# Hash-masked attention with a gated MLP: engine order written by hand, packed operand transposes, weights loaded late

## The chip, the cores and the metric

One core of one Trainium2 chip runs the whole program. The metric is device time in microseconds (us) of one execution. In the profile PE is TensorE (matmul), PEld its weight loads, DVE is VectorE, ACT is ScalarE, POOL is GpSimd; SPq is the queue on which the sync engine issues DMA transfers. "PEclk" or "clock" is the share of full clock that TensorE was granted. "Fast" and "slow" are the states of an execution; only fast ones are compared unless the text says otherwise. L190 is line 190 of the kernel in question, so line numbers differ from kernel to kernel.

## The reference, cut to what matters

```python
batch, n_heads, seq, head_dim = (4, 8, 768, 64)
q_bits = (np.einsum('bhsd,dk->bhsk', q, proj) > 0)       # 6 hash bits a token
k_bits = (np.einsum('bhsd,dk->bhsk', k, proj) > 0)
mask = q_bucket[:, :, :, None] == k_bucket[:, :, None, :]
scores = np.where(mask, scale * np.matmul(q, k.transpose(0, 1, 3, 2)), -1e9)
x = softmax(scores) @ v                                  # heads side by side: 3072 x 512
# gated MLP with residual
gelu = gelu_erf(x @ w_gate)                              # 512 -> 1536
ffn_out = (gelu * (x @ w_val)) @ w_out                   # 1536 -> 512
out = x + sigmoid(x @ w_res) * ffn_out
```

Both kernels hold the mask in the matmul: each operand of a score gets seven more rows, six hash bits as plus or minus 0.5 and a constant, so that equal buckets add nothing and unequal ones a large negative number. The work goes by pairs of heads, 16 in all, four to a batch. A pair has nine score chunks; I call one chunk, with its exponential and the value matmuls of the chunk before, a slot. A batch has 36 slots. Its gate/value block (`x @ w_gate`, `x @ w_val`, some 31 us of pure TensorE) comes four slots into the next batch, five in the changed kernel, and for the last batch at the end. The output rows of a batch (`rps`, `fps`) are cut into 30 pieces and slipped between the slots of the next batch. Meanwhile two pairs ahead are prepared: a group.

## The kernel before

The preparation makes one 128x1536 tile an operand, holding data and bits, and transposes it by DMA. All hash matmuls of a group go into one PSUM tile `hs`, and the bits are written before the transpose:

```python
def prep(ps, first=False):
    jobs = [(p, side) for p in ps for side in range(2)]
    hs = mm_ps.tile([P, HT, 32], FP32, tag="mm", name="hs")
    ...
    for h in range(2):
        ...  # VectorE transposes 32x32 blocks of q, k into tt
        for dh in range(2):
            for j, tt in enumerate(t32):
                nc.tensor.matmul(hs[32 * j:32 * j + 32, h * T:(h + 1) * T, :],
                                 projw[:, dh, :], tt[:, :, dh, :], ...)
        yield
    nc.vector.transpose(ht..., hs...)
    for j, x in enumerate(jobs):
        for a in range(4):
            nc.vector.tensor_scalar(nat_of(x)[32 * a:32 * a + 32, :, D:D + NBITS], ht..., ...)
        nc.sync.dma_start_transpose(out=ag, in_=nat_of(x)...)
        aug[x] = ag
        yield
```

The main loop issues a chunk, one step of the preparation, one piece of a row; the tile scheduler orders the engines from there. Weights are loaded from the first slots on:

```python
    scores(p, c)
    ...
    if s in (3, 6, 9, 12, 15) and g < 3:
        load_w()
    next(side, None)
    if b >= 1:
        ...  # one projection piece a slot
        if slot == LEAD - 1:
            ...
            gate_val(b - 1)
```

The row's PSUM tiles `rps` and `fps` and the hash tile share one pool of two buffers: `mm_ps = tc.tile_pool(name="mm_ps", bufs=2, space=PSUM)`.

The softmax here doesn't subtract the row's maximum and nothing guards it: scores larger than these inputs give would overflow.

## Time and profile before

| | before |
|---|---|
| time | 410.14 us median of 2 runs (408.52 to 411.77) |
| profiled execution | span 404.7 us, mean clock 0.920 |
| first score | 21.7 us |
| gate/value block of batch 0 | 98.2 to 132.3 us |
| batch 1, batch 2, batch 3 (from the end of one block to the end of the next) | 84.8, 84.0, 78.1 us |
| after the last block | 25.5 us |

The span is the end of block 0, plus three batches, plus a tail of 25 to 26 us. The profile lines are in the prediction.

### The profile page before, as it was taken

To read this page: it belongs to the slowest core of one execution; us is meant where nothing else is said; L and a number is where in the kernel's file an instruction comes from. 1 tells how busy PE (TensorE), PEld (TensorE's weight loads), DVE (VectorE), ACT (ScalarE), POOL (GpSimd) and SP (SyncE) were. 2 spreads that over 40 slices of the span, in tenths; PEclk is the share of its full clock that TensorE was granted. 3 is DMA by queue.
4 is the path that set the end of the run, shared out by engine and by line. 5 is a ranking of instruction groups with operands and counts; after the bars stand their busy time and mean duration, and the time that the engine had idled before them with its cause. 6 is when DMAs were issued, how large, how long until landed. Compare 5 with 4: busy or idle time off the path is not lost. (4 is left out here: it accounts for less than half of the span.)

```text
span 404.7 us, 7265 instructions
## 1 busy us (share of the span) xinstructions
PE 366.9 (91%) x2944; PEld 202.2 (50%) x2990; DVE 170.7 (42%) x366; ACT 206.9 (51%) x225; POOL 81.5 (20%) x149
## 2 busy tenths in 40 slices
PE   6386969959999999998999999899999999999995
PEld 2133524425566555554665555556655555565542
DVE  3727123715433324734336537443336232333342
ACT  2036534636332877773335886863357788333210
POOL 7456245344300022241000342310000000000000
PEclk9759555865999999999999999999999999999999
DMA  7999999996910048776000973920008221100012
GB/s 220 223 270 245 159 239 285 201 238 142 238 55 2 28 84 188 137 186 202 2 0 2 185 205 85 185 47 2 0 2 158 76 68 47 45 2 0 16 65 78
DMA packets 86177, 46.61 MB, mean 115 GB/s; under 512 B 64640, under 2 KB 83072, under 8 KB 86144
## 3 DMA queue, kind: packets, MB, share of 16 engines
q1 hardware_dynamic: 79488, 40.91, 44.7%
q0 software_dynamic: 6336, 5.24, 8.7%
q8 instruction: 23, 0.38, 0.4%
q14 instruction: 10, 0.08, 0.1%
q10 hardware_dynamic: 320, 0.01, 0.0%
HBM read 29.37 MB, written 6.29 MB: 88 GB/s over the span
## 5 line engine op out<-in xcount | busy, mean ns | idle before, releaser
L260 ACT ACTIVATE e<-sp 128x1024 bf16<-128x1024 f32 x144 | 144.4, 1022 | 83.8 <-PE sp L255 82.4
L255 PE MATMUL sp<-aug,aug 71*128 71x256 bf16 (+1 forms) x384 | 98.2, 362 | 4.3 <-DMA aug<-nat 4.1
L282 ACT ACTIVATE gt<-sp 128x768 bf16<-128x768 f32 x48 | 38.9, 810 | 83.3 <-PE sp L276 83.3
L283 DVE TENSOR_TENSOR hh<-gt,sp 128x768 bf16<-128x768 bf16 x48 | 45.8, 953 | 81.1 <-PE sp L276 81.1
L235 PEld LDWEIGHTS <-e 128*128 128x128 bf16 x1152 | 54.3, 104 | 43.1 <-ACT e L260 24.0
L276 PE MATMUL sp<-x_sb,wg 128*128 128x512 bf16 (+1 forms) x382 | 72.0, 328 | 2.6 <-DMA x_sb<-x_tok 2.1
L300 PE MATMUL fps<-wo,hh 128*128 128x512 bf16 x265 | 71.4, 379 | 1.7 <-issue 0.5
L276 PE MATMUL sp<-x_sb,wv 128*128 128x512 bf16 (+1 forms) x371 | 70.0, 324 | 1.2 <-DVE hh L283 0.5
L235 PE MATMUL av<-va,e 128*128 128x65 bf16 x1152 | 66.1, 204 | 2.2 <-ACT e L260 1.1
L168 DVE STREAM_TRANSPOSE t<-ld 128x384 f32<-128x384 f32 x64 | 33.8, 557 | 43.8 <-DMA ld<-in_q_dram 21.3
L276 PEld LDWEIGHTS <-wg 128*128 128x128 bf16 x384 | 37.5, 98 | 28.1 <-issue 3.9
L255 PEld LDWEIGHTS <-aug 71*128 71x128 bf16 x384 | 34.8, 105 | 32.4 <-issue 6.5
L276 PEld LDWEIGHTS <-wv 128*128 128x128 bf16 x384 | 37.7, 98 | 25.8 <-issue 1.2
L175 PE MATMUL hs<-t,projw 128*32 128x192 f32 x256 | 27.3, 375 | 17.8 <-DVE t L168 11.7
L300 PEld LDWEIGHTS <-hh 128*128 128x128 bf16 x288 | 24.3, 97 | 24.0 <-issue 5.3
L305 DVE SCALAR_TENSOR_TENSOR o<-th,fps 128x512 f32<-128x512 f32 x24 | 16.4, 683 | 39.4 <-PE fps L300 29.6
L186 DVE TENSOR_SCALAR nat<-ht 32x72 bf16<-32x72 f32 x128 | 31.3, 244 | 2.3
L214 DVE RECIPROCAL rec<-av 128x6 f32<-128x6 f32 x32 | 6.0, 187 | 56.0 <-PE av L235 56.0
L138 POOL TENSOR_SCALAR nat<-ld 128x768 bf16<-128x768 f32 x15 | 12.4, 829 | 73.8 <-DMA aug<-nat 73.8
L296 ACT ACTIVATE th<-rps 128x512 f32<-128x512 f32 x24 | 14.3, 596 | 21.0 <-PE rps L293 17.7
L145 POOL CAST va<-ldv 128x768 bf16<-128x768 f32 x16 | 13.2, 822 | 57.2 <-PE av L235 52.5
L293 PE MATMUL rps<-wr,x_sb 128*128 128x512 bf16 x88 | 24.3, 382 | 0.1
(34 smaller groups left out, 152.9 us busy)
## 6 DMA issues: line engine op xcount, KB each, us to landing
ld<-in_q_dram SPq DMA_DIRECT2D x16, 384.0 KB, 4.7
ld<-in_k_dram SPq DMA_DIRECT2D x16, 384.0 KB, 4.6
ldv<-in_v_dram SPq DMA_DIRECT2D x16, 384.0 KB, 5.0
out_dram<-o SPq DMA_DIRECT2D x24, 256.0 KB, 2.1
wg<-in_moe_w_gate_dram POOLq DMA_DIRECT2D x4, 384.0 KB, 9.6
wv<-in_moe_w_val_dram POOLq DMA_DIRECT2D x4, 384.0 KB, 7.1
wo<-in_moe_w_out_dram POOLq DMA_DIRECT2D x3, 512.0 KB, 10.7
aug<-nat SPq DMA_TRANSPOSE x32, 4.9
```

The lines of the kernel that those rows point to most:

```text
L168: nc.vector.transpose(tt.rearrange("p c h n -> p (c h n)"), raw[x][:, h * T:(h + 1) * T].rearrange("p c d -> p (c d)"))
L175: nc.tensor.matmul(hs[32 * j:32 * j + 32, h * T:(h + 1) * T, :], projw[:, dh, :], tt[:, :, dh, :], start=(dh == 0), stop=(dh == 1), tile_p ...
L186: nc.vector.tensor_scalar(nat_of(x)[32 * a:32 * a + 32, :, D:D + NBITS], ht[32 * j:32 * j + 32, :, NBITS * a:NBITS * (a + 1)], 0.0, 0.5, o ...
L235: nc.tensor.matmul(av[p, hi][:, qt, :], e[:, off:off + P], va[:, hi, jt, 0:D + 1], start=False, stop=(jt == T - 1), skip_group_check=True)
L255: nc.tensor.matmul(sp[:, off:off + nq * P], ks[0:KA, hi * T + jt, :], qs[0:KA, hi * T + qt0:hi * T + qt0 + nq, :], start=True, stop=True)
L260: nc.scalar.activation(e, sp, AF.Exp, scale=float(ALPHA))
L276: nc.tensor.matmul(sp[:, c0:c1], w[:, kk, bass.ts(m, P)], xs[:, kk, c0:c1], start=(kk == 0), stop=(kk == KM - 1))
L282: nc.scalar.activation(gt, sp[:, 0:S], AF.Gelu)
L283: nc.vector.tensor_mul(hh[:, m, :], gt, ps[1][:, 0:S])
L293: nc.tensor.matmul(rps, x_sb[b][:, kk, t, :], wr[:, kk, :], start=(kk == 0), stop=(kk == KM - 1))
L300: nc.tensor.matmul(fps, hh[:, m, bass.ts(t, P)], wo[:, m, :], start=(m == 0), stop=(m == KF - 1))
L305: nc.vector.scalar_tensor_tensor(o, th, 1.0, fps, op0=ALU.add, op1=ALU.mult)
```

## The change

Its intent: fewer and smaller DMA transposes, no waits in the first stage, and every engine's order written down instead of left to the scheduler. Two heads share a 128x768 transpose. The second head lands in rows 64 to 127, so VectorE copies it into a tile `second` whose first 64 rows hold its mask rows and zeros. Bits go in by small DMAs ("mask rows") after the transpose. Hashing uses 32x32 tiles, in blocks of 16 matmul instructions that need both buffers of `mm_ps` (the trace records each of them twice, so a block shows as x32). Weights are loaded at slots 20 to 40.

```diff
+    ctx.enter_context(tc.manual_schedule(engines=None))
 ...
+    def move_second(x):
+        nc.vector.tensor_copy(second[x[0] % NM][x[1]][D:P], aug[x][D:P])
 ...
+    def hash_mm(jobs, h, a0):
+        while rows_open:
+            mlp_piece()
+        hs = [mm_ps.tile([P, T, 32], FP32, tag="mm", name="hs") for _ in range(2)]
+        for dh in range(2):
+            for j, x in enumerate(jobs):
+                for i in range(2):
+                    a = a0 + i
+                    nc.tensor.matmul(hs[i][32 * j:32 * j + 32],
+                                     projw[32 * a:32 * a + 32, dh, :],
+                                     t32[x, h][32 * a:32 * a + 32, :, dh, :],
+                                     start=(dh == 0), stop=(dh == 1),
+                                     tile_position=(32 * a, 32 * j))
 ...
+    def mask_rows(jobs, h, sel=None):
 ...
+            dst = aug[x][D:D + NROW] if h == 0 else second[x[0] % NM][x[1]][0:NROW]
+            nc.sync.dma_start(dst, bits[jobs[0]][32 * j:32 * j + NROW, h])
 ...
+        at(s0 + 6, hash_mm, jobs, 0, 0)
+        at(s0 + 7, hash_bits, jobs, 0, 0)
+        at(s0 + 7, hash_mm, jobs, 0, 2)
+        at(s0 + 8, hash_bits, jobs, 0, 2)
+        for i, x in enumerate(jobs):
+            at(s0 + 8 + i // 2, blocks, x, 1)
+            at(s0 + 9 + i // 2, move_second, x)
+        at(s0 + 11, mask_rows, jobs, 0)
+        at(s0 + 10, hash_mm, jobs, 1, 0)
+        at(s0 + 11, hash_bits, jobs, 1, 0)
+        at(s0 + 11, hash_mm, jobs, 1, 2)
+        at(s0 + 12, hash_bits, jobs, 1, 2)
+        at(s0 + 13, mask_rows, jobs, 1)
 ...
-            if s in (3, 6, 9, 12, 15) and g < 3:
-                load_w()
+    for s in (20, 22, 28, 30, 36, 37, 38, 39):
+        at(s, load_w)
+    for s in (40, 40, 40, 40):
+        at(s, load_w)
 ...
+            elif mlp and mlp[0][1] < 5 * T - HELD:
+                mlp_piece()
```

`at(slot, f, ...)` puts a piece of work into a slot; within a slot the order is scores, the listed work, a row piece, then the values of the chunk before. `s0` is the first slot of a group's preparation, 18 slots before its use (15 for the first group).

## The prediction

> **What bounds the kernel now.** I read the page first: busy shares, the 40 slices, the clock row.
>
> ```profile
> PE 366.9 (91%) x2944; PEld 202.2 (50%) x2990; DVE 170.7 (42%) x366; ACT 206.9 (51%) x225; POOL 81.5 (20%) x149
> PE   6386969959999999998999999899999999999995
> ACT  2036534636332877773335886863357788333210
> PEclk9759555865999999999999999999999999999999
> DMA  7999999996910048776000973920008221100012
> ```
>
> TensorE is the busy engine, but the clock row splits the run: for some 100 us it is mostly at half speed, then full to the end. In the first part DMA is full too. The table of 10 us stretches and the DMA queue's timeline say more (columns: length, then busy us and instructions of PE, PEld, DVE, ACT, POOL; clock, DMA share, GB/s).
>
> ```profile
> 40.00:50.00 10.00, 9.89 (x70) 5.05 (x71) 1.93 (x6) 5.12 (x5) 1.59 (x3) 0.50 1.33 166
> 60.00:70.00 10.00, 10.00 (x72) 4.14 (x70) 2.91 (x8) 4.81 (x5) 5.83 (x10) 0.50 1.16 268
> 150.00:160.00 10.00, 9.89 (x110) 5.70 (x109) 4.64 (x10) 7.30 (x8) 2.74 (x5) 1.00 0.68 117
> 50.13 10.44 SPq L191 DMA_TRANSPOSE aug<-nat  x2
> ```
>
> Five exponentials in 10 us early, with TensorE "99% busy" at clock 0.50; later 8 of them plus the projections. Two operand transposes hold the queue for 10.44 us, and loads queue behind them.
>
> Stage limits come from the timeline of TensorE and the chain that ended last.
>
> ```profile
> 98.18 0.83 PE L276 MATMUL sp<-x_sb,wg 128*128 128x512 bf16 x2
> 132.17 0.60 PE L255 MATMUL sp<-aug,aug 71*128 71x256 bf16 x3
> 216.93 0.60 PE L255 MATMUL sp<-aug,aug 71*128 71x256 bf16 x3
> ...
> 301.10 0.43 PE sp L255 x3
> 348.20 1.57 PE sp L276 x9
> 379.28 2.54 PE fps L300 x11
> ```
>
> So: batch 0 with its gate/value block ends at 132.2 (first score at 21.7, block from 98.2); batches 1 and 2 take 84.8 and 84.2; batch 3's attention 47.1; then 31.1 of block and 25.4 of tail. From 132 on TensorE is the bound, nearly without gaps. Its unit costs at full clock, from the chain:
>
> ```profile
> 263.78 1.29 PE fps L300 x6
> 265.07 0.44 PE sp L255 x3
> 265.51 0.24 PE av L235 x8
> ...
> 267.73 0.79 PE hs L175 x16
> ...
> 392.57 0.40 issue
> 392.96 0.70 DVE o L305
> 393.66 0.04 issue
> 393.70 2.75 PE fps L300 x12
> ```
>
> One score chunk (a "slot") is 0.44 + 0.25 = 0.69 us of TensorE and one exponential of 0.99 us (3.97 for four in a row at 78.52). A projection matmul is 0.216. The last four lines show the cost of a full PSUM pool: from the end of one row (392.53) to the next start it is 1.17 us, because VectorE must first read the bank.
>
> **What the Trainium skill says.**
> - "TensorE: Matmul & The Clock Gate", Part 1, has a half/full clock set by activity in free-running windows of about 3.4 us. The trace agrees in kind: half clock at 15.2 after idling from 10.4 to 14.0, full again at 28.9, four windows later. It also warns of a throttle that sticks; here 40 to 73 us stays at 0.50 although TensorE hardly idles.
> - Same page, Part 3: 32x32 tiles run together, about 4 ns apart, and Part 1 ("Wait — 56ns, not 53.3ns?") gives a floor of about 25 ns from start to start. Before, four column tiles overlap: 16 recorded hash matmuls in 0.79 us.
> - "TensorEngine Tiling (Array Packing)", Gotcha 1: different row tiles need different PSUM banks. No run here shows it yet, but it explains why the new hash takes two tiles.
> - "DMA: Bandwidth & Descriptors", Anatomy: about 2 us fixed per transfer. Here a 256 KB output lands in 2.1 us (median), so the new small mask-row transfers should take about that.
>
> **The change part by part.**
>
> *Transposes.* 32 DMA transposes of 128x1536 become 28 of 128x768, the first two pairs go through TensorE (24 small ones), and VectorE copies half of each result. The old ones took 2 to 5 us of queue each; the same half-size transpose for x_sb takes 1.2 us of queue. Together with the late weights this removes the DMA bound of stage one. 64 small mask-row DMAs (about 0.45 us to issue) come in. VectorE loses 128 bit writes of 0.244 and nine transposes (36 us) and gains some 72 bit writes (I take 0.3) and 28 copies (about 0.3): near 30 us. It is at 42%, so neither counts.
>
> *First score.* projw lands at about 7 to 8 us as before. Four hash blocks of pair 0 then run serially, since each takes both buffers of the small PSUM pool and waits for VectorE: about 0.85 + 0.8 each, 6.6 in all. Then transposes, two blocks of pair 1 and twelve more transposes precede the first score in TensorE's order: some 6 us. First score at about 21, against 21.7: nothing won.
>
> *Stage one.* 41 slots, gate/value block after slot 40. At full clock the exponential sets the slot: 41 x 1.0. Eight hash blocks in four neighbouring pairs add about 1.3 per pair, 5; mask rows of pair 2 issued only two slots before use, plus a few microseconds at half clock: 5. Block at 21 + 51 = 72, its end at 72 + 31.4 + 1.5 = 105. Before: 132.2. **Minus 27.** If the clock sticks at half: 41 x 1.36 (the exponentials at 47.56, 48.92 and 50.21 have that spacing) = 56, hash blocks of 1.5 and seeds 18, so the end is at 128: minus 4. I expect full clock (70%)[...].
>
> *Batches 1 to 3.* This is where I part from the intent. Hash tiles are 32x32 instead of 128x32, so there are four times as many; 32 recorded matmuls per block, estimated at 1.1 us (ideal 0.8; by the 25 ns floor for matmul plus load more). Two groups of four blocks make 8.8 per batch against about 2.8. Worse, each block needs both small PSUM buffers, so the code first drains the open projection row. TensorE's order in a batch, from the built program (S score, F fps, R rps, H hash, A values, V seed):
>
> ```
> slot 5: S R4            slot 10: S F6 H16 R4 V A4 V A4
> 6, 7: S F12 H16 R4 A8   11: S F12 H16 R4 A8
> 8, 9: S F3 A8           12-14: S F3 A8
> 15-23: S A8             24: S F3 H16 A8   25, 28, 29: S H16 A8
> 26, 27, 30-35: S A8     next 0-2: rest of the row; 3, 4: S A8
> ```
>
> The 24 projection pieces, once spread over 24 slots, are used up in ten. Sum, slots 5 to 14: 1.3 + 3 x 5.24 + 5 x 1.34 + 4.29 = 28.0; stalls at four hash blocks: 1.17 (bank still read for the row) + 0.55 (rps waits for the bits) each, 6.9; 34.9 in all, with ScalarE starved. Slots 15 to 23: bound by exponentials, 9.0, TensorE idle 30%. Slots 24 to 29: 10.7. Slots 30 to 35: 6.0. Slots 0 to 4 of the next batch: 7.6. Total 68.2 + 31.4 of block = 99.6, against 84.5: **plus 15 twice.** Batch 3: 34.9 + 21 slots x 1.0 + 5.5 = 61.4 against 47.1: **plus 14.** Tail unchanged.
>
> Net: 410 - 27 + 44 = 427; with the clock stuck 450.
>
> **The rivals.**
> 1. *The start wins all.* If row tiles overlap ideally (0.82 per block) and VectorE answers in 0.9 us, a batch loses 9 rather than 15, in all 28; a first score at 19 and 48 us of slots give minus 34. Then 404. For it: the old hash overlaps perfectly. Against it: the drain order and the imbalance stand in the program whatever a block costs.
> 2. *Hash matmuls bound by issue.* At 50 ns per load and matmul (0.79 / 16) a block takes 1.6 us: about 4 us more per batch, 438 or above.
> 3. *The half clock persists* through stage one: about 450. For it: 40 to 73 us before. Against: more rows active, no long DMA waits.
> 4. *DMA still rules stage one.* Loads of eight pairs (9.4 MB) and 6.3 MB of weights at the 250 to 280 GB/s of the early slices are 60 us, within the 72 available, and the later weight pieces are not needed until the block is well under way. A few us at worst.
>
> **Range and chances.** The main line gives 427, stuck clock 450, the optimistic 404. I took long estimates for the stalls, so I set 424, with 400 to 450 for 8 in 10. Faster by over 2% (below 402) needs rival 1 and more: 0.17. Within 2%: 0.28. Slower: 0.55.
>
> **What would show it.** The clock row should be nearly all 9 from slice 3 on and the block should start at about 72. The hash line should have 1024 matmuls, and blocks of about 1.1 us. In slots 6, 7, 10 and 11 of batches 1 to 3 TensorE should wait about 1.2 us for VectorE's o and 0.5 us for the bits; the slices after them should show TensorE near 7 and ScalarE at 9 with full clock. Batches 1 and 2 should take about 100 us each. I am wrong if they take 85 to 90, which would mean the stalls or the imbalance are hidden, or if the block starts before 62 or after 90.

## The result, and the profile after

The changed kernel took 460.05 us (459.24 and 460.85), against 410.14: ratio 1.1217, interval 1.1007 to 1.1426. A ratio is the mean time of one kernel's fast runs over that of the other's of the same rounds, so it is not quite the quotient of the medians.

| | before | predicted | after |
|---|---|---|---|
| first score | 21.7 | 21 | 25.3 |
| end of block 0 | 132.3 | 105 | 133.7 |
| batch 1, 2, 3 | 84.8, 84.0, 78.1 | 99.6, 99.6, 92.5 | 101.1, 101.4, 95.4 |
| span | 404.7 | | 457.5 |

(The predicted 92.5 is its 61.4 of attention and 31.1 of block.) The spans differ by 52.8 us: 1.4 to the end of block 0, 16.3, 17.4 and 17.3 in the batches, 0.4 in the tail. So the predicted loss in the batches is there, and the predicted gain of stage one isn't.

From the page of the changed kernel, the same rows as in the prediction:

```profile
PE   7688855739998888899998888899999887799996
ACT  2066750832351466772353276663244178623211
PEclk9998995968999999999999999999999899999999
DMA  6239699899002265481002167360001102100011
```

The clock row is now nearly all full, as expected, and yet block 0 ends later. The holes are in the PE row, its sixth to ninth digit (5, 5, 7 and 3; 57 to 103 us), just where the DMA row shows 9, 9, 8 and 9; ScalarE falls to 0 in one of them. Early on, the DMA row has a 2 and a 3, room that nobody uses.

The DMA queue's timeline of the changed kernel (start, length, line, form) has two groups of four equal operand transposes, one before and one after the first weight load is issued at 52.9 us:

```profile
34.33 5.82 SPq L173 DMA_TRANSPOSE aug<-nat  x4
...
54.95 15.04 SPq L173 DMA_TRANSPOSE aug<-nat  x4
```

The second takes 15 us instead of 6. And from the chain that ended last (start, length, what):

```profile
56.53 16.16 DMA aug<-nat
...
73.75 1.95 PE hs L216 x24
...
88.99 11.45 DMA x_sb<-x_tok
...
100.48 0.80 PE sp L335 x2
```

Two DMA transfers stand on the path that sets the end, 27.6 us together. On the first one waits a copy on VectorE, behind it stand block transposes of VectorE, and on those waits the hash block that TensorE has next in its order, 9.4 us long (first line of the table of waits below). During that wait the clock falls to half, from 68 to 82 us. On the second waits block 0 itself: x's last part is transposed beside the weight pieces issued from 86.3 to 90.8 us.

In the batches the pattern that the program's order had promised is there, again from the chain:

```profile
135.44 2.16 PE fps L362 x10
...
138.15 0.70 DVE o L367
...
138.89 0.97 PE hs L216 x30
139.86 0.41 DVE bits L232
...
140.32 1.02 PE rps L354 x4
```

A row is pulled to its end, VectorE reads its bank for 0.70 us, then the hash block may start, then the next row waits for the bits. The table of waits sums them up (us in all, times, longest):

```profile
PE hs L216 <- DVE t L191: 11.6, 2, 9.4
...
PE rps L354 <- DVE bits L232: 6.6, 12, 0.6
PE hs L216 <- DVE o L367: 6.5, 14, 0.7
```

And when the pieces are used up, ScalarE is the bound (five of its exponentials run back to back from 371.88 us, 5.09 us together): in this stretch of batch 3 (length, then PE, PEld, DVE, ACT, POOL; clock, DMA share, GB/s) TensorE is at 7.8 and ScalarE at 8.2 of 10 us.

```profile
370.00:380.00 10.00, 7.79 (x97) 4.27 (x97) 1.42 (x4) 8.21 (x10) 0.00 (x0) 1.00 0.20 22
```

### The profile page after: what moved, and what is told of

Same layout as the page of the kernel before. It is cut to its first block, busy times and chain, and to the rows that moved or that the text cites. A ratio compares the mean times of both kernels' runs of the same rounds, so it can differ in the third digit from the quotient of the medians.

```text
span 457.5 us, 8891 instructions
## 1 busy us (share of the span) xinstructions
PE 387.5 (85%) x3717; PEld 211.3 (46%) x3776; DVE 171.7 (38%) x334; ACT 209.5 (46%) x229; POOL 83.1 (18%) x155
## 4 chain that ended last, share of the span: by engine, by line
PE 66%; DVE 10%; DMA 8%; ACT 8%; issue 5%; SPq 1%; POOL 1%; ACTq 0%; DVEq 0%
PE sp L335 27%; PE fps L362 10%; PE hs L216 8%; PE sp L316 8%; ACT e L320 8%; PE av L297 5%; PE rps L354 5%; DMA aug<-nat 4%; DVE bits L232 3%; DMA x_sb<-x_tok 3%; DVE o L367 2%; DVE x_tok L276 2%; DVE t L191 2%; DVE second L178 1%; PE av L290 1%
## 5 line engine op out<-in xcount | busy, mean ns | idle before, releaser
L297 PEld LDWEIGHTS <-e 128*128 128x128 bf16 x1152 | 51.3, 99 | 62.5 <-ACT e L320 46.6
L297 PE MATMUL av<-va,e 128*128 128x65 bf16 x1152 | 63.8, 197 | 18.4 <-ACT e L320 16.5
L335 PE MATMUL sp<-x_sb,wg 128*128 128x256 bf16 (+1 forms) x377 | 71.2, 329 | 7.4 <-DMA x_sb<-x_tok 7.1
L335 PE MATMUL sp<-x_sb,wv 128*128 128x256 bf16 (+1 forms) x376 | 70.9, 328 | 0.6 <-issue 0.2
L216 PE MATMUL hs<-t,projw 32*32 32x192 f32 x1024 | 50.4, 357 | 23.8 <-DVE t L191 11.6
L316 PE MATMUL sp<-aug,aug 71*128 71x512 bf16 x192 | 56.8, 337 | 0.0
L316 PE MATMUL sp<-second,second 128*128 128x256 bf16 (+1 forms) x166 | 46.2, 326 | 0.3 <-DMA second<-bits 0.2
L216 PEld LDWEIGHTS hs<-t,projw 32*32 32x32 f32 x1024 | 23.0, 110 | 49.4 <-issue 12.1
L362 PEld LDWEIGHTS <-hh 128*128 128x128 bf16 x288 | 28.2, 98 | 33.8 <-issue 3.2
L232 DVE TENSOR_SCALAR bits<-hs,cst 128x192 bf16<-128x192 f32 (+1 forms) x72 | 26.7, 411 | 30.4 <-PE hs L216 30.3
## 6 DMA issues: line engine op xcount, KB each, us to landing
wv<-in_moe_w_val_dram POOLq DMA_DIRECT2D x4, 384.0 KB, 10.5
aug<-bits SPq DMA_DIRECT2D x32, 10.5 KB
```

The costliest lines, as they stand in the source:

```text
L216: nc.tensor.matmul(hs[i][32 * j:32 * j + 32], projw[32 * a:32 * a + 32, dh, :], t32[x, h][32 * a:32 * a + 32, :, dh, :], start=(dh == 0), ...
L232: nc.vector.tensor_scalar(bits[jobs[0]][:n, h, :, 32 * a:32 * a + 32], hs[:n], 0.0, cst[:n], op0=ALU.is_gt, op1=ALU.add)
L297: nc.tensor.matmul(av[p, hi][:, qt, :], e[:, off:off + P], va[:, hi, jt, 0:D + 1], start=False, stop=(jt == T - 1), skip_group_check=True)
L316: nc.tensor.matmul(sp[:, off:off + nq * P], ks[0:n, jt, :], qs[0:n, qt0:qt0 + nq, :], start=True, stop=True)
L335: nc.tensor.matmul(sp[:, c0:c1], w[:, kk, bass.ts(m, P)], xs[:, kk, c0:c1], start=(kk == 0), stop=(kk == KM - 1))
L362: nc.tensor.matmul(fps, hh[:, m, bass.ts(t, P)], wo[:, m, :], start=(m == 0), stop=(m == KF - 1))
```

## The experiments

Theory A: the late weight loads share the DMA engines with the operand transposes of stage one and with x's, and that costs what the change was to gain. Its rival C: the copies of the second heads stand too early in VectorE's order, and the wait would be there at any DMA speed. Theory B: in the batches, the order (rows drained before each hash block, pieces used up, VectorE's order) costs the time, not the hash work itself.

All runs in one table; the kernel before, run beside each set, had medians from 406.04 to 409.83 us.

| run | end of block 0 | batch 1, 2, 3 | span | time |
|---|---|---|---|---|
| after | 133.7 | 101.1, 101.4, 95.4 | 457.5 | 460.05 |
| s1_no_weight_dma | 114.0 | 101.8, 101.2, 93.8 | 436.6 | 438.36 (fast one) |
| s2_move_later (slow profile) | | | 462.1 | 457.31 (fast one) |
| s2b_move_and_rows_later | 133.1 | 103.6, 103.1, 93.9 | 459.5 | 461.95 |
| s3_wr_wo_after_x | 130.7 | 101.7, 101.3, 93.8 | 453.3 | 457.66 |
| s4_weights_early | 114.9 | 101.3, 102.8, 95.5 | 440.3 | 442.33 |
| s5_late_hash_off | 134.4 | 85.9, 84.7, 79.8 | 410.7 | 412.48 |
| s6_drain_only | 132.0 | 88.8, 88.8, 83.9 | 419.3 | 423.43 |
| s7_no_open_row | 140.0 | 100.6, 96.5, 87.7 | 450.6 | 450.29 |
| s8_both | 112.9 | 98.0, 98.3, 88.7 | 423.7 | 424.87 |
| s9_both_and_copies_last | 113.4 | 95.2, 94.9, 85.3 | 414.6 | 417.44 |
| s10_filled_start | 115.1 | 94.7, 98.0, 85.5 | 419.2 | 420.19 |
| s11_spaced (slow profile) | 117.2 | 96.8, 98.4, 87.0 | 425.3 | 414.69 (fast one) |
| s12_rows_after_ends | 116.4 | 96.8, 95.1, 82.8 | 416.9 | 418.89 |
| s13_queue_order | 112.2 | 89.1, 89.5, 82.8 | 399.4 | 401.21, 405.35 (fast ones) |

The batches are differences of rounded block ends, so a last digit can be off by one. Three runs leave stage one as it is in the changed kernel (133.7): s5, s6 and s7. Their 134.4, 132.0 and 140.0 show how far the end of block 0 moves by itself; a few us of it prove nothing.

### Stage one

**No weight loads.** The weights are filled with a constant instead of loaded. Its output is wrong, which doesn't matter for the time.

```diff
-            nc.gpsimd.dma_start(*wload.pop(0))
+            nc.gpsimd.memset(wload.pop(0)[0], 0.03)
```

> The changed kernel with its twelve weight loads replaced by constants that GpSimd writes at the same places (wrong result on purpose). Theory A: the block of batch 0 starts at 100 us instead of my 72 because the late weight loads share the 16 DMA engines with the operand transposes (15.0 us of queue for four at 54.95) and with the last x_sb transpose (11.5 us to land). Then four transposes take about 6 us, x_sb lands in about 3, and the block runs from about 80: total near 440. Rival B: the transposes and pair loads are slow by themselves, or VectorE's order is at fault: the block still starts after 95 and the total stays above 455. Batches 1 to 3 should stay at about 101, 101 and 64.

Block 0 started at 82.2 us and ended at 114.0, 19.7 earlier; the batches stayed. The same group of transposes on the DMA queue:

```profile
55.52 5.48 SPq L173 DMA_TRANSPOSE aug<-nat  x4
```

That is 15.04 us with the loads beside it and 5.48 without. Theory A holds for some 20 us. GpSimd's own time for issuing the loads, another suspect, is not it: the memsets that stand for them took it longer (1.38 us for a gate or value piece, against 0.75 to 0.97 to issue one). The first score stayed at 25.25, and 9 us to the predicted 105 stay too.

**Copies later.** The rival, by moving `move_second` behind the hash work.

```diff
-            at(s0 + 9 + i // 2, move_second, x)
+            at(s0 + 12 + i // 2, move_second, x)
```

> The changed kernel with VectorE's copies of the second head moved three slots later, behind the block transposes and bits of their group. Theory C: the 9.4 us hash wait at 63.8 comes from VectorE's fixed order, the copy waiting for its DMA transpose and holding back block transposes that are ready: the wait goes, and the block starts 6 to 10 us earlier, total near 452. Rival: the late transpose only delays something else (the mask rows or the scores of pair 4 wait for it), and the total moves by less than 3.

The result was wrong. The mask rows of the first head, still sent at slot `s0 + 11`, land in rows 64 to 70 of the transposed tile, and the copy now read them there instead of the second head's data. Mended, the first heads' mask rows go after the copies:

```diff
-            at(s0 + 9 + i // 2, move_second, x)
-        at(s0 + 11, mask_rows, jobs, 0)
+            at(s0 + 12 + i // 2, move_second, x)
+        at(s0 + 14, mask_rows, jobs, 0)
```

> s2 mended: the copies of the second head at slots 12 and 13 of a group, and the first head's mask rows after them at slot 14, since those rows overwrite what the copy reads (s2 was wrong for that reason). Correct. Theory C: the 9.4 us hash wait of batch 0 goes and the block starts 5 or more earlier, and in batches 1 to 3 VectorE's bits no longer stand behind copies; total near 450. Rival: total within 4 of the changed kernel's 460.

Correct, and no faster (461.95; ratio 1.1327, 1.1241 to 1.1413). Block 0 ended at 133.1. TensorE now waited 2.2 us for block transposes instead of 11.6, and for the mask rows instead (us in all, times, longest):

```profile
PE sp L316 <- DMA aug<-bits: 14.5, 4, 7.3
```

The rival falls: the order of the copies decides where the wait appears, and the transposes' length that it appears.

**Only the last weight pieces later.** `wr` and `wo` are loaded after x's transpose has landed, by a tiny GpSimd copy that reads it.

```diff
-    for s in (40, 40, 40, 40):
-        at(s, load_w)
+    def after_x():
+        nc.gpsimd.tensor_copy(junk, x_sb[0][:, HP - 1, 0, 0:1])
+        for _ in range(4):
+            load_w()
+    at(40, after_x)
```

> The changed kernel with wr and wo loaded only after the last x_sb transpose of batch 0 has landed (GpSimd reads one element of it first). Theory A2: GpSimd runs ahead of the slots, so loads written for slot 40 start at 87.8 us and share the engines with the x_sb transpose issued at 89.0; with them away it lands in about 4 us instead of 11.5 and the 7.1 us wait shrinks to about 1, total near 453. Rival: the transpose waits for the gate and value weights and pair loads that are still in flight, and the wait stays above 5.

Block 0's wait for x fell from 7.1 to 5.2 us only, as the rival of this run had it. Its end went from 133.7 to 130.7, which is not clear of the spread above: at most the small part.

**Weights early.** Five pieces are loaded in the start and three in slots 0 to 2, where the DMA row had room; `wr` and `wo` as above. The result is correct.

```diff
     cast((1, 1), nc.gpsimd)
+    for _ in range(5):
+        load_w()
 ...
-    for s in (20, 22, 28, 30, 36, 37, 38, 39):
-        at(s, load_w)
+    for s in (0, 1, 2):
+        at(s, load_w)
```

> The changed kernel with five gate/value pieces issued in the start, when the DMA engines idle (10 to 18 us at share 0 to 0.09), three at slots 0 to 2, and wr and wo after the x_sb transpose. Theory A: the first scores move by at most 2 us, group 2's transposes no longer meet weight loads, the block starts at about 80 and the total is near 440. Rival: the loads of pairs 2 and 3 and the mask rows are delayed instead, the first score slips to 30 or more, and the total stays above 450.

442.33 us, ratio 1.0809 (1.0653 to 1.0965). Block 0 ended at 114.9, nearly as early as with no loads at all, and the four transposes took this long:

```profile
57.85 6.33 SPq L173 DMA_TRANSPOSE aug<-nat  x4
```

So the same bytes cost 19 us at slots 20 to 40 and next to nothing at the start. That settles theory A.

The Trainium skill, "DMA: Bandwidth & Descriptors", section "Queues, rings and completion order", says that each DMA engine takes turns between the queues that have work, a packet at a time. The two lengths, 15.04 and 5.48 us, agree with a queue that must share; how the turns went no run here shows.

### The batches

**No hashing for pairs 6 to 15**, and no draining; a constant mask tile, so wrong on purpose.

```diff
+        if jobs[0][0] >= 6:
+            bits[jobs[0]] = fixed
+            return
         while rows_open:
             mlp_piece()
```

> The changed kernel without the hash matmuls and bits of pairs 6 to 15 and without the drain of the projection rows before them; the mask rows come from a constant tile (wrong result on purpose). Batch 0 as before it, its block ends near 134. My step for batches 1 to 3 says the hash blocks with their drain, waits and imbalance cost 15, 15 and 14: batches 1 and 2 then take about 84 and batch 3 about 49, span near 407. Rival: the batches are slow for another cause (interleaved heads, both value buffers freed at once, small mask-row DMAs): they stay above 92.

Batches of 85.9, 84.7 and 79.8 us: within 2 us of before. The kernel before still hashes in them (2.6 us of TensorE in batch 1, 3.9 in batch 2), so whatever else changed there (one exponential a chunk of both heads, smaller transposes, hand order) costs a few us a batch at most. Of the 51.0 us that three batches lost, 47.5 go with hashing and the draining for it.

**Draining alone**: as above, but rows are pulled to their end where the hash blocks were.

```diff
+        while rows_open:
+            mlp_piece()
         if jobs[0][0] >= 6:
             bits[jobs[0]] = fixed
             return
-        while rows_open:
-            mlp_piece()
```

> As s5, but the open projection row is still drained at the four hash places of each group. This parts the imbalance from the hash blocks and their waits. My ledger without the blocks and waits gives 52.5 for the attention part, so about 85 per batch: the drain alone is worth 1 to 3 per batch over s5, and the rest of the 15 to 17 is the blocks (about 6.5 instead of 2.8) and the waits for VectorE around them. Rival: the imbalance is the main thing, and batches take 92 or more.

88.8, 88.8 and 83.9: the imbalance costs 11.1 us in the three batches, more than expected (two stretches of 3.4 us at half clock, at 171.6 and 260.4, are part of it). The other 36.4 (297.9 less 261.5) come with the blocks and what waits for them.

**No open row at a hash block.** Row pieces get slots of their own, so that no block has to drain one; the blocks of the later groups one slot earlier. Correct.

```diff
+        d = 1 if g >= 3 else 0
-        at(s0 + 6, hash_mm, jobs, 0, 0)
+        at(s0 + 6 - d, hash_mm, jobs, 0, 0)
 ...  (the other blocks likewise)
+    PIECES = {14: 2, 18: 2, 22: 2, 31: 2, 33: 2, 35: 2}
+    for i in (11, 12, 13, 15, 16, 17, 19, 20, 21, 29, 30, 32, 34):
+        PIECES[i] = 1
 ...
-            elif mlp and mlp[0][1] < 5 * T - HELD:
-                mlp_piece()
+            else:
+                for _ in range(PIECES.get(slot, 0)):
+                    mlp_piece()
```

> The changed kernel with the hash blocks of batches 1 to 3 at slots where no projection row is open and the 25 pieces put between them, so that nothing is drained and no hash block waits for a row's bank (correct). If the waits around drained rows are the cost: batches 1 and 2 fall from 101 to about 88, batch 3 from 63.8 to about 53, span near 420. If the hash blocks themselves and the bits' waits are the cost: they stay above 95.

100.6, 96.5 and 87.7: far less than expected. The waits of rows and drains were gone, and a new one stood there, in the timeline of TensorE:

```profile
149.57 1.85 PE L216 MATMUL hs<-t,projw 32*32 32x192 f32 x32 [2.43 <-DVE bits L232]
```

The fourth block of a group waits 2.43 us for the bits of the third, because VectorE has copies of second heads ahead of them in its order; then the clock is at half, and the block takes 1.85 us instead of 0.9.

**Both mends together.**

```diff
+    for _ in range(5):
+        load_w()                                # as in the run with weights early
 ...
+        at(s0 + 6 - d, hash_mm, jobs, 0, 0)     # as in the run with no open row
 ...
+    PIECES = {14: 2, 18: 2, 22: 2, 31: 2, 33: 2, 35: 2}
```

> s7 with the weights early as in s4 (correct). If the two losses add: 440 less 37, about 403 span, at or just below the kernel before. Rival: the savings overlap or the early part limits later loads, and it stays above 415.

424.87 us, ratio 1.0448 (1.0362 to 1.0535). The 21 us of block 0 and the batches' gains add up, but 403 was expected of them, and the batches stayed at 98, 98 and 89.

**Copies behind all bits** in the later groups, and the first heads' mask rows behind the copies; correct.

```diff
-            at(s0 + 9 + i // 2, move_second, x)
-        at(s0 + 11, mask_rows, jobs, 0)
 ...
+        if g > 1:
+            for x in jobs:
+                at(s0 + 13, move_second, x)
+            at(s0 + 14, mask_rows, jobs, 0)
 ...  (the second heads' mask rows go to slot 14 too)
```

> s8 with the copies and the first head's mask rows of groups 2 to 7 behind all of the group's bits (correct). In s7 the last hash block of each group waited 2.4 us for bits that stood behind copies and block transposes in VectorE's order, and TensorE's clock fell to half after it. If that is what kept s7's batches at 96 to 100 instead of my 88: batches of 88 to 92, span near 408. Rival: the wait only moves to the block transposes and batches stay at 96.

417.44 us, ratio 1.0256 (1.0179 to 1.0333): 9.6 us gained in the batches (285.0 to 275.4), and not the whole of the expected. TensorE still waited for bits, since two blocks follow each other in neighbouring slots.

**A filled start.** Three dummy matmuls after each hash block and transpose of the start, to keep the clock up.

```diff
     hash_mm(jobs0, 0, 0)
+    filler(3)
     hash_bits(jobs0, 0, 0)
```

> s9 with three dummy 512-column matmuls behind each hash block and transpose of the start (correct). In the changed kernel the six hash blocks of the start take 1.82 us each at half clock, against 0.85 for the same block at 28.4. If the clock is the cause, the blocks take about 0.9 and the first score comes at about 20 instead of 25, the total falls by 4 to 5. Rival: the chain is bound by VectorE's bits and the loads, and the first score moves by less than 1.5.

The first score came at 21.96 instead of 24.69 us, and hash blocks of the start took 0.85 to 1.21 us instead of 1.82. So the cold clock is what made the first score late. But block 0 started at 82.8 against 81.7: the 2.7 us did not reach it. The time was 420.19, no better.

**A slot between blocks.** Blocks at slots 5, 7, 11 and 13 of a group; rows at slots 8 and 9, then from 14 on; weights early. The copies stand at slot 10 of a group in this edit and the next two, after the first heads' bits; the recorded text says after the last bits, which the edit does not do.

```diff
+        o = (6, 7, 10, 11) if g == 1 else (5, 7, 11, 13)
+        at(s0 + o[0], hash_mm, jobs, 0, 0)
+        at(s0 + o[0] + 1, hash_bits, jobs, 0, 0)
 ...
+    PIECES = {8: 2, 9: 3, 14: 1, 15: 1, 16: 1, 17: 2, 18: 1, 19: 1, 20: 1, 21: 2,
+              26: 2, 27: 3, 32: 2, 33: 3}
```

> Early weights as before, and the hash blocks of the later batches at slots 5, 7, 11 and 13 of each group's sixteen, one slot without a hash block between them, copies after the last one's bits. If the wait of a hash block for the previous block's bits is what keeps the batches of the version with copies last at 95 us (TensorE waits 12.2 us for them in all, about 4 a batch), the batches come to about 91 us and attention of the last to about 50, the span to 403 to 410, and the time to within 2% of the kernel before. Rival, that the batches are held by the hash blocks' and transposes' own work on TensorE and VectorE beside slots that ScalarE bounds: batches stay at 94 to 96 us and the span at 412 to 417, whatever the spacing.

Three of four runs were slow, the profiled one too; the fast one took 414.69. It is inconclusive as a time. Its trace still tells what happened to the waits (us in all, times, longest), first of the version with copies last, then of this one:

```profile
PE hs L216 <- DVE bits L232: 12.2, 11, 1.7
```

```profile
PE av L290 <- DVE rec L275: 11.8, 9, 1.7
...
PE hs L216 <- DVE bits L232: 3.7, 5, 1.7
```

The wait for bits is gone, and one of the same size came: the values of a new pair wait for the reciprocals of the old, which on VectorE stand behind the two output operations of a row that ends in that slot. And such a pause can cost twice, as two neighbouring 6 us stretches show (columns as above):

```profile
153.00:159.00 6.00, 4.17 (x38) 2.09 (x36) 3.55 (x9) 2.36 (x3) 0.00 (x0) 1.00 0.43 126
159.00:165.00 6.00, 5.78 (x84) 3.05 (x91) 1.68 (x6) 2.81 (x3) 0.00 (x0) 0.52 0.29 62
```

After a stretch with TensorE at 4.17 of 6 us the clock is at half. This profile is slow, and the half clock may be what makes it slow, so I take no size from it.

**Rows end one slot later**, behind the reciprocals.

```diff
-    PIECES = {8: 2, 9: 3, 14: 1, 15: 1, 16: 1, 17: 2, 18: 1, 19: 1, 20: 1, 21: 2,
-              26: 2, 27: 3, 32: 2, 33: 3}
+    PIECES = {9: 3, 10: 2, 14: 1, 15: 1, 16: 1, 17: 2, 18: 1, 19: 1, 20: 1, 21: 2,
+              27: 3, 28: 2, 32: 2, 33: 3}
```

> As the version with spaced hash blocks, with the output row that ended in the slot where a pair's last values are drained now begun in that slot and ended in the next. If the 11.8 us in which TensorE waits for the reciprocals come from VectorE's two output operations standing in front of them, that wait falls to about 3 us, so 3 us a batch, the pause of some 2 us in which the clock falls to half does not come, the batches come to 91 to 93 us, the span to 403 to 409 in a fast run, and the time to within 2% of the kernel before. Rival, that the wait only moves again (to the copies' or the bits' order on VectorE): the waits sum to what they were, and the span stays at 412 to 416 in a fast run.

418.89 us: the rival was right. The wait for reciprocals fell to 0.7 us, and this one stood in its place:

```profile
PE sp L316 <- DMA second<-bits: 14.3, 6, 3.7
```

The DMA queue's timeline says why:

```profile
127.92 0.36 SPq L371 DMA_DIRECT2D out_dram<-o  x1
128.33 2.71 SPq L281 DMA_TRANSPOSE x_sb<-x_tok  x1
131.13 2.98 SPq L240 DMA_DIRECT2D aug<-bits  x4
...
135.72 3.03 SPq L240 DMA_DIRECT2D second<-bits  x4
```

The transfers left in the order of the program. The first heads' mask rows stand behind the store of a row and x's transpose, the second heads' behind those and three loads; the next pair's scores wait for them.

**The queue's order.** The first heads' mask rows go one slot earlier, before the row's store, and the loads behind the second heads' mask rows. Correct.

```diff
-        at(s0 + 11, mask_rows, jobs, 0)
+        at(s0 + (11 if g == 1 else 10), mask_rows, jobs, 0)
-            at(s0 + 12, load, pb + 2, (0, 1))
-            at(s0 + 13, load, pb + 2, (2,))
+            at(s0 + 15, load, pb + 2, (0, 1))
+            at(s0 + 15, load, pb + 2, (2,))
```

> As the version before, with the first heads' mask rows sent ahead of the output row's store, and three loads behind the second heads' mask rows. If the queue's order is what delays the mask rows, TensorE's wait for them falls from 14.3 us in six places to under 4, the batches come to 91 to 93 us, attention of the last to about 50, the span to 402 to 408, and the time to within 2% of the kernel before. Rival, the wait moves once more (say to the loads of values or the half clock): the span stays at 412 to 417.

Its two fast runs took 401.21 and 405.35 us, its two slow ones 407.40 and 408.59; before took 404.72 to 410.64 in its six fast runs. The ratio is 0.9958, interval 0.9867 to 1.0050: the same as before, with no proof of more. The page and the longest wait of TensorE:

```profile
PE   6687887789999999899999999899999998999995
...
PEclk8559999999999999999999999999999999999998
```

```profile
PE av L297 <- ACT e L320: 10.1, 20, 0.7
```

Batches of 89.1, 89.5 and 82.8. From 113 to 374 us, the batches alone, TensorE waits 5.2 us for ScalarE's exponentials and 1.5 us for all else. This time the wait did not move on. From the changed kernel to this one the span lost 58.1 us: 21.5 to the end of block 0, and 12.0, 11.9 and 12.6 in the batches (the 0.1 left is tail and rounding), with all the same work done.

## Why the prediction was right or wrong

Its direction was right, its mechanism in the batches too, and the gain of stage one, and with it the size, was wrong: 424 was said, 460 came out.

**First score at about 21: wrong, 25.3.** The term that was too small is the hash block of the start. It took 1.82 us, not 0.85, as TensorE was at half clock. The filled start shows that: 21.96 with warm blocks. It hardly matters, as those 2.7 us did not survive to block 0.

**"Stage one ... Minus 27": the step that failed; measured plus 1.4.** The prediction said of the transposes: "Together with the late weights this removes the DMA bound of stage one." The late weights were that bound. The step leaned on dismissing rival 4, "DMA still rules stage one ... A few us at worst", by dividing all bytes by the rate of the early slices. The sum of bytes was not the question. The weight loads came from 52.9 us on, just when the transposes that the next slots needed were on the queue, while the room of the first 35 us stayed unused. Nor was the rate reached: the page's GB/s row shows 149 to 209 from 34 to 103 us, where the sum took 250 to 280. The prediction compared totals over 72 us and did not ask which transfer each slot waits for. By the prediction's own test, a start of block 0 after 90, it fell: the first matmuls came at 92.3 and, after a wait for x, the block went on at 100.5. With no weight loads block 0 ends at 114.0, with early ones at 114.9: 19 to 20 of the 28.7 us between 105 and 133.7. Of the 9 left without loads, 4.3 are the late first score by count, and 6.3 the slots with hash blocks: in s1 these eight took 19.3 us from exponential to exponential, 11.3 over 1.0 each, where the prediction allowed 5. The block itself was 1.2 us shorter than said. This is a count and no experiment (the 2.7 us that the filled start won were lost again before block 0), so the cause of these 9 stays open; even the last version, at 112.2, is 7 us behind the 105.

**"I expect full clock (70%)": right.** After the start, the clock row is full outside the holes that the DMA waits make, but for two stretches of 3.4 us (from 41.0 and 358.4). Why the kernel before stayed at half speed from 40 to 73 us isn't answered by any run; that TensorE "hardly idles" there is not quite so, since it waits 3.4 us before 55.15.

**"Plus 15 twice", "plus 14": right, a little short; measured 16.3, 17.4 and 17.3.** The ledger by slots held. In batch 1, from exponential to exponential, slots 5 to 14 took 33.2 us (34.9 said), 15 to 23 10.0 (9.0), 24 to 29 12.1 (10.7) and 30 to 35 6.1 (6.0). Inside the first of these, two terms were too long: most hash blocks took 0.88 to 0.97 us in the chain, not 1.1, and the stalls for VectorE's `o` and the bits 13.1 us in all or 4.4 a batch, not 6.9. The terms that were too short are the slots from 15 to 29. That the slots after it would be bound by ScalarE is right (8.2 against 7.8 of 10 us).

**VectorE "is at 42%, so neither counts": wrong as a reason.** VectorE was no busier than before (171.7 us against 170.7), but TensorE waited for it in every batch, and moving its work in its order was worth 9.6 us (copies last).

**"The drain order and the imbalance stand in the program whatever a block costs": right as a sentence, and half the story.** The three batches lost 51.0 us to before; 36.5 of them were order (297.9 us before the mends, 261.4 after the last, with the same hashing). About 11 are left over the version without hashing (250.4); hash blocks fill 8.6 us of batch 1 in the last version, 10.8 in the changed kernel and 2.6 before. So rival 1 did describe what this change can be: its loss of 9 a batch is more than the 4.3 to 5.5 that the last version shows. But not as the change was written.

**The rivals that named the clock or a bound by issue** (450 and 438): neither happened.

What stays open: the last 7 to 9 us of stage one; the clock of the kernel before; and how much of s11's half clock was the slow state of that run.

## What to carry to other kernels

Before calling a transfer hidden, list for each stage which transfers share the engines with the one that the next step waits for, and when; a sum of bytes over a stage shows only that they would fit. A hand-written order fixes every queue at once, so a wait mended on one engine appears on the next one (here bits, then reciprocals, then mask rows, then little): follow it by the table of waits until little is left but waits for one that is itself near its bound. And taking away a suspected cost entirely, even with a wrong result, sized each part in one run.

## What the Trainium skill lacked or had wrong

- "DMA: Bandwidth & Descriptors", Rules for kernel authors, says that a transpose next to ordinary DMAs needs nothing. That is about right results. What it costs in time is missing: four 128x768 transposes took 15.04 us beside weight loads and 5.48 without.
- No page gives a queue time measured on this chip for small transfers: four mask-row DMAs of 10.5 KB each took 3.0 us of the issuing queue (2.98 and 3.03 above), so 0.75 each, more than the 0.38 to 0.50 of most 384 KB loads there, and everything behind them waited.
- "TensorE: Matmul & The Clock Gate", Part 1, HAM oscillation, puts the rule as no idle gaps over some 3.4 us; the page also speaks of short, frequent idle times that do the same, without a length. In s7, TensorE paused three times for 2.43 us in the batches, and each time the clock was at half within 2 us of the pause's end; after two of them the block took 1.85 us instead of 0.9.
- The same page, Part 1, Seeing it yourself, warns that clock events in a trace can be unreliable. They can be missing, and the page of a run then shows full clock: the changed kernel's trace has no clock record before 27.3 us, its row has 9 for the first 34 us, and its hash blocks of the start took 1.82 us, twice the warm 0.85; the last version's row has 5 from 10 to 30 us with the same 1.82. The length of a known block is the check.
